# Block-sparse attention with a gated convolution feed-forward on one core: more buffers in eight pools, and another written-out order

## The chip, the cores and the metric

The kernel runs on one core of a Trainium2 chip. The metric is the device time of one execution in microseconds (us); lower is better. Three runs of the kernel before gave 210.2, 214.19 and 211.23 us, a median of 211.23 us.

## The reference

The input is q, k and v of shape (4, 8, 768, 64), a table of three random key blocks for each of the 24 query blocks, and the weights of a feed-forward layer. Cut to what matters:

```python
mask = (abs(blk_i - blk_j) <= 1) | first or last block | sampled blocks   # blocks of 32
scores = where(mask, q @ k.T / sqrt(64), -1e9)
attn = softmax(scores)                         # over the keys
x = (attn @ v) as (4, 768, 512)                # heads side by side
h = maximum(x @ w_in, 0)                       # 512 -> 1024
conv = sum over k of conv_w[k] * h shifted by k - 1 along the sequence
out = (h * sigmoid(conv)) @ w_out              # 1024 -> 512, float32
```

## The kernel before

The attention is computed densely: the mask comes in through 24 extra rows of the contraction (64 + 24 = 88 partitions), so that masked scores get a large negative term. Queries and keys are kept transposed in tiles `e` and `o` (the two heads of a pair, lines 326 and 328 for the copies into them). The scores of a unit, eight blocks of 128 by 128, are written by TensorE into one of two PSUM tiles `st` (L744). ScalarE takes their exponential into a tile `pt` (L755). TensorE multiplies `pt` with the values `vt`, which carry a column of ones, into one of two PSUM tiles `av` (L777). There are 144 such units. When a pair of heads has all its keys, VectorE takes the reciprocal of the row sums (L694) and normalizes into `xtok` (L696); a DMA transpose issued by SyncE (L705), or in a few places TensorE (L715), gives the transposed tokens `xT`.

The feed-forward runs on segments of 384 tokens (the last two of 256 and 128) between the units of later segments. TensorE multiplies `xT` with `winb` into a PSUM tile `mix` (L893). ScalarE (L913) or VectorE (L915) applies the relu into `hE`. VectorE does the convolution with per-partition weights `cw` (L947 and L957), ScalarE the tanh (L996), VectorE the gate `gT` (L999 and L1004). TensorE multiplies `gT` with `woutb` (L823; L808 for the last block), ScalarE (L326) or VectorE (L328) evicts into `o2s`, and a DMA writes the output (L831, L817). In the last segment the convolution is done on TensorE (L968) with diagonal matrices `diag` that VectorE writes (L388).

The loads of the first pair of heads come through SyncE and ScalarE in float32 and are cast (L238, then L326 or L328). All other loads of q, k, v and the large weights are issued by GpSimd, which converts while loading; a small copy named `pace` (L415 and L658) makes GpSimd wait for a unit's `pt` or for an earlier load. The pairs from number 5 on are transposed by DMA into `stg` (L583) and copied. The convolution weights are loaded as `cw0`, 24 rows of 128, by one small DMA (L238); TensorE transposes them (L378) and VectorE writes `cw` (L380).

The program is first built as a graph of operations, each with the engines that may do it and the pools from which it takes buffers. Then `put_down` reads the string `ORDER`. Each entry is two characters that number an operation, one for the engine where there is a choice, and one for each buffer that it takes:

```python
o = ops[64 * CODE.index(line[x]) + CODE.index(line[x + 1])]
...
for b in o.allocs:
    b.index = CODE.index(line[x])
```

So the string decides the order on every engine's queue, which engine does a copy, an eviction or a relu, and which buffer is used. Every engine runs its instructions in the order of its queue, and the waits between them follow from the data and the buffers.

Of the kernel before, what the change touches and what calls it, by code (L numbers as in the profile page):

```python
# [21 lines left out]
rmrnrorprqrrrsrtru0Y0rv1210ZA00XA0VA0+ArwrxryrzrArBrCrDrErFrGrH0/015110A16A0i0x13V14V0lV0jVrI4o017A0y0mV11V0B
0nA4prJrK4t14q04u1g11hV11j01lV1kV0q0p1dV01E21G31H1801m11S00O1U2461V0t0u0w0v4v11iV4y04z4D14E4A24I04J4F34K44r14s
4w4Q14R4S54x4B4C0s0r1rV14V04W4G1u01vV24+14/4X05011x11zV4H4L1yV4N0530544M05b15c4T0E15525d31wV0C0F1FV25g05h1I04U
5l14Y5i45m1JV34Z1L11KV5n51MV1NV4O5q05r19051525v15w565s05x1571TV30G5810J0N591bV1aV5e15D05E5f5j5k5o5I15J5F25p5t
1n15N05u5y5O5z05G0P470Q48241490R4a1A04b0S4c2604d274e0T4f2c24g1O14h2e14i2f4j2k04k2m34P05a4l2n4m5K35S15H5L5T5P4
5A25B5C1oV5U55/05M605Q6105R6415V5W656906a5X05Y25V41pV5Z05+V6616e16216fhr1ho06b26g36j0hp636khs0k0DhqV0htVhM06l4
6r1676s6t5hx0hyhzA6w06xhu1hv1B06y0hOhNhPhwVhQhU1hVhWhX6B16C686c6d6hhD16G0hE6H1CA1DA6D1hFAhA06i6m6n06O1hB1W16u
6P6v6z6I2hCAhRhY1XV46o1i021YV6pi16Q36T0hG06A6U6E6V4hH6F6Y16ZhJ16J6+56KhK710726R16S6WhZhLAhIA730i3hSi26L0i4hT0
i57611P1im06X6/1RV1QV777e01Z1707f747817j17k756M2806q1296Ni831+V1/Viah+2dV0h/i9ig17g27l37o07p797a07h7i7t17u7q4  # L30
i6ibi77b2ic7v5ih7B07C7D0id7m7n7r7s7G17w7x7Hin2lV12aV0io7L07M2g12h7I17N2ii7c7d7y12bV7z7E17Q17R7F7J7K7V07Wieifip
7O7S37A7X42s12u2v24n0IiqV0811827P7T7U860878358807Y7Z0ij8b18civ0iw8g08h7+02iV12jV2tV2ixV7/ikA1is1itiuViQ08d12o0
2p8i28o18p8q3iB08t0848uiC858v48y18z898a8e8f8D08E8j8kiy1iz8A58F12x2w2C2002F802iAAiRiSiTiDViU2qV2iV2rV8l2iY1iE0
8r18s8I18w8JiF8K0iGA8x8Q02118B8R8C8V18W8GiH0iI8H8S28X3iZi+22V8miW23Vi/8+08/904iXj0iJVj18LiK1iL931948M0iMVj42j5
8N1j7j28O8T9b08U8Y9ciN0iO8Z91iPVj39559g19h9d19i0jC19l09m9n3929697980jc3j6jdj8jfjejg999q19r9s59e19f9j9k9v09wjq0
9x19D19E9o9pjr9t9u9I0jD9y9J9z0j99F0jh9N19G9O9HjajbjijEjs9K59P02G02D22EV3jj2I2H2Q2N2R12O02y12z2J08n2K8P9a9S09T
jFjt9U2juA20L2LV39A2jGV32PV49B2MV2AV40K2BV9+19L9M9/a30a49QjI1jJa04jL0a819RjM9Va9a53jKA1jNA2/3032T2S2Yaa032ad0
aejU19Wa119X19YjX0k40jVai1a2jYaf1jWAk6jZVa6a7ajk11aq0abark2jO0acak2jPas5k5kk1k7kmjQAav1awaA0agahalaBjR0jSam0
ax4aC3k8k3Vklknan0j+1j/k0VkoaF1atjTAk9kc2aokdks3kfkakektkgkukb1aGaN0jk0auayaOaH0jlazaS1aTaP1kpaU5jw1jmaX0aYir
jHjv2U09C0il331aZ4khjxaDaEjnjoA0aIaJb01b1b23jyjzb50aQ1aRb6aVaWkA0jAA3b70kqaK22V2WV0kvkikwkjaLkxbd1a+bekG1a/b3  # L40
b4kBbi0bjkHb8b902Z131373820Map9Z34aMbf2bn1bo2XVkykrkCkzkD2+V0bk139V135V1bp536Vba0bb3a3b23f3c3d3ebs0kIbtkJkKV2
bA1kEA1kP0bBkQkM1kNkRVkOVl80l9lalblcbu4bC3bF0bGbgbhblbK1bLbmkS0bqbH0bM2bP0brbQkTbR1bU1kV1kWbVc00bvbwbD1bEc1ld
kUVkXVbx1lg2lhlelibyk/0bIbJbNbW5c23c51c6c70bOl0ca0cbbSbTbXbY0cf1cgkY1kZcc2ch5ljl1Vlklfk+VbZ2lllo13p3m3n03q03u
3r3g0bc1jp3hkFb+b/bzc3l20c4cn0cocp4l51l3l6cs1ctcx0l4Al7Acyc8c9lK0cdcecicjcu1cz3lplqlr3v1lw3lmlxlnlslylzcC1cD
cE0ltck0lAlucllvlE1cq1cH0lFcIcP1crcvcwcAcQcBcFlLcGcJ5cU0cKcL0cVlGlMlBcR4cW13s3E3t3B3F13J3G3H3C13I3Q3R2cmcScZ1
c+3iV2lClDlHlNd20d3cTc/2cXda1db3oV2lIV0cM2lOV1d43dc0m31cYd0m00d1m1m4cN3jVm2V0m5Adf0dgdk1dlm60m7dh5mo0mpm8Vdm4
mf1mgd5d6dp0dqdu1mc0mddr1meAmhAdd1jB3w3klP3K0cO23L3T3U33Y3V3W3Xdvdw2434403ldedC0dDml0mmm91mamnAdE3mr3xV4d71mq
3yVmsmE2dH1didImi0mjmFmGmbVmw1mxdJ0mkVmtd8djdM0dndodNlQ1dR1dSdslRdO5lSdtdxdZ0d+lTdT4mM3mHmz3DV3dz0mumydAmImv0
mAlUV3mNmOd/1e21e3dy0dFdGdKe70e42dLlW0lXdPdQe8ec1dUdVedmJmBe93lYlZe01m+1e1ee0mCdW2mDmPl+A1eh0eiej5e5e6m/eamU0
mVebep1eqeu0evmKmQdXmLmR3MV3mSmTn0mWn13Z1kL3+d93SV445V03/V0mXefegekdBlVdYl/3AlJer4ew1n2A2em13NVen40VmYA3ez1eA  # L50
eE0nd1eFeB2neeG3na0nbnfVncVnA0nBnCnDnE3PmZ3O3z41eo042eM1eNeO0el0n41eR0eSeT5n5n70n8eW1eseteXe/0exeyf0eCeDn6An9A
ns1eY4ng1nhf41eHeIf5nj0f11nFntnuniVeJ0nveKf62fc0nkfdfe3nwnlVnxnGnI2np1nqnJnrVnKnynLeP1fh1eQfinm0eUeVfm0eZfnnn
e+f2f3f7fj0fo5noAnznMnQ3nSnRnHf92nTfafr1f80fffsfgfkflfpfz0fAft4fB1nNnY1fE1fFo20fqfufvfJ0fKfG2fw1nUnOfL3nVfxnP
nZo3fR1fC1fDfHfSfIfMfW0fXfNn+o4fT0fY5eLfbfyf/1fU0g0nWg14nXo5o6V10Hg70g8n/fVfZgc1gdo0A0ok0olo7n3o1g91ge2fO0omV1
on1ooopVoI1oKgh0gioq0gp1gj3oJoLfPot1orosAgqouovAoQ0oRoToSgu0gvgr0oC0f+g2oF1oGoHAoDoEAgw5g3g42oUp42g5ga1gbgz1gA
oz1oAgfgggkglow0oxoBAgB4p5gm1oMgs0gnoyAoY3gtgxgyfQ1g6gogCgI0gJgDoNgN1gK1gOoe1ofogp6gE0gFoZo+gL1gG0gMgV0gP2gHV
o/oVp0oOoWohgQgWp7oP1gS2oiA3gR0po0ppgX3pqApA1gTp8h11h2pu1gYgZpvpx0pyh60h30pwApr1pspzAp1pBpCoXpQ0p2p3g+0pDg/ptA
p9papRpEpbpI3pJpLo80o9h7gU2h0hf1oaobhgh41h5h85ocA1pi1pjpkhh4plh9ha0hihjpc0pmA2pFhb1hchd1heAhk2pKhlpdpehm1pfpM
pNpgA0pGhnVqg1qhqiAqp0qqpHpY2pSpOpTqrAqj1qkqs1qtqm0qnqlAqu1qoAqx0qypPqz3pZp/pUpVp+qvq0phpnodojq1qa1qC1q40qDqH0
# [1001 lines left out]
```

## Time and profile before

| quantity | value |
|---|---|
| median of three runs | 211.23 us |
| span of the profiled execution, first to last instruction | 207.2 us |
| the profiled execution's own total time | not shown on the page; the median is 4.0 us above the span |
| TensorE busy | 196.7 us, 95% |
| ScalarE busy | 189.4 us, 91% |
| VectorE busy | 181.5 us, 88% |
| GpSimd busy | 60.7 us, 29% |
| granted TensorE clock | 1.000 |
| loads and stores | 26.26 MB, mean 127 GB/s |

Busy times are read with care. An instruction's time runs from its start to its end, and neighbours on one engine overlap by a little, so that the sum of busy times is more than the time that the engine needs. A matmul that is held up counts as busy too. In the rows of the profile, PE is TensorE's matmul, PEld its weight load, ACT is ScalarE, DVE VectorE, POOL GpSimd, SP SyncE; a q behind the name stands for the issue of a DMA. Rows of the timeline give the start, the duration, the engine, the line, the operation and the count of instructions that were merged; what stands in brackets is the idle time before and what ended it. The DMA share is the mean busy share of 16 DMA engines by the times of their packets, and it can exceed 1 where packets of several queues overlap on an engine.

### The profile page before, as it was taken

The numbers are of one execution on the slowest core, as the hardware profiler recorded it, in microseconds if no ns is written. First come the engines' busy times: TensorE is split into PE (matmuls) and PEld (weight loads), VectorE is DVE, ScalarE is ACT, GpSimd is POOL, SyncE is SP. The second block draws the span as 40 slices with busy tenths as digits, with TensorE's granted clock in tenths as the row PEclk, the third lists the DMA queues.
The fourth block names the chain that finished last, engine by engine and source line by source line (L and its number), as shares of the span: only waits on it lengthen the run. The fifth ranks groups of instructions, "written<-read, shape, count | busy, mean of one in ns | idle before, by whom it ended". The sixth has DMA issues, their size and how long they took to land.

```text
span 207.2 us, 6783 instructions
## 1 busy us (share of the span) xinstructions
PE 196.7 (95%) x2667; PEld 153.7 (74%) x2687; DVE 181.5 (88%) x571; ACT 189.4 (91%) x248; POOL 60.7 (29%) x113
## 2 busy tenths in 40 slices
PE   7799979989999999999999999999999999999993
PEld 7689858867878877777688767777688877795752
DVE  6877759999699998999999998999799959999950
ACT  6899969999999999999999998999899999998841
POOL 8844355446326124500605292700000000000000
...
GB/s 149 170 207 200 173 169 126 141 135 157 158 151 134 98 138 194 181 190 58 77 167 133 88 103 218 170 213 73 175 43 22 19 121 66 29 11 6 156 50 202
DMA packets 54903, 26.26 MB, mean 127 GB/s; under 512 B 40864, under 2 KB 51832, under 8 KB 54872
## 3 DMA queue, kind: packets, MB, share of 16 engines
...
## 4 chain that ended last, share of the span: by engine, by line
PE 56%; ACT 16%; DVE 16%; DMA 5%; issue 4%; SPq 0%; ACTq 0%
PE st L744 16%; PE mix L893 14%; PE mix L823 14%; ACT pt L755 12%; PE av L777 9%; DVE m L947 5%; DMA xT<-xtok 3%; DVE m L957 3%; DMA o2s<-in_q_dram 2%; DVE hE L915 2%; DVE xtok L696 2%; DVE gT L1004 1%; ACT hE L913 1%; DVE m L999 1%; DVE e L328 1%
## 5 line engine op out<-in xcount | busy, mean ns | idle before, releaser
L755 ACT ACTIVATE pt<-st 128x1024 bf16<-128x1024 f32 x144 | 140.2, 1036 | 5.4 <-PE st L744 5.0
L777 PEld LDWEIGHTS <-pt 128*128 128x128 bf16 x1152 | 53.1, 97 | 11.6 <-issue 0.2
L777 PE MATMUL av<-vt,pt 128*128 128x65 bf16 x1152 | 60.6, 193 | 0.3
L893 PE MATMUL mix<-xT,winb 128*128 128x384 bf16 (+2 forms) x288 | 53.8, 308 | 1.1 <-DMA xT<-xtok 0.9
L947 DVE TENSOR_SCALAR m<-hE,cw 128x382 bf16<-128x382 bf16 (+2 forms) x192 | 49.6, 317 | 0.2
L744 PE MATMUL st<-o 88*128 88x128 bf16 (+1 forms) x240 | 44.3, 229 | 1.1 <-ACT pt L755 0.8
L744 PE MATMUL st<-o,e 88*128 88x128 bf16 (+1 forms) x228 | 43.8, 233 | 0.5 <-ACT pt L755 0.4
L744 PE MATMUL st<-e,o 88*128 88x128 bf16 (+1 forms) x224 | 43.0, 234 | 1.2 <-ACT pt L755 1.2
L823 PE MATMUL mix<-woutb,gT 128*128 128x512 bf16 x156 | 43.1, 379 | 0.8
L744 PE MATMUL st<-e 88*128 88x128 bf16 (+1 forms) x208 | 41.5, 239 | 0.6 <-ACT pt L755 0.5
L744 PEld LDWEIGHTS <-o 88*128 88x128 bf16 x464 | 34.4, 97 | 9.4 <-issue 3.0
L744 PEld LDWEIGHTS <-e 88*128 88x128 bf16 x436 | 33.0, 97 | 7.5 <-issue 1.4
L957 DVE TENSOR_TENSOR m<-m 128x764 bf16<-128x764 bf16 (+2 forms) x64 | 33.8, 532 | 0.4
L893 PEld LDWEIGHTS <-winb 128*128 128x128 bf16 x288 | 23.9, 97 | 8.2 <-issue 1.6
L996 ACT ACTIVATE m<-m 128x764 bf16<-128x764 bf16 (+2 forms) x32 | 26.3, 826 | 0.5 <-DVE m L957 0.4
L415 POOL COPY pace<-pt 1x1 bf16<-1x1 bf16 x24 | 8.3, 347 | 47.3 <-ACT pt L755 47.0
L823 PEld LDWEIGHTS <-gT 128*128 128x128 bf16 x184 | 15.4, 97 | 9.0 <-DVE gT L1004 0.5
L915 DVE TENSOR_SCALAR hE<-mix 128x384 bf16<-128x384 f32 x29 | 15.9, 554 | 4.3 <-PE mix L893 4.1
L696 DVE TENSOR_TENSOR xtok<-av,rcp 128x384 bf16<-128x384 f32 (+2 forms) x36 | 18.2, 506 | 0.3
L1004 DVE TENSOR_TENSOR gT<-m,hE 128x764 bf16<-128x764 bf16 (+3 forms) x36 | 18.1, 508 | 0.3
L913 ACT ACTIVATE hE<-mix 128x384 bf16<-128x384 f32 (+2 forms) x35 | 16.9, 503 | 1.6 <-PE mix L893 1.2
L238 POOL DMA_DIRECT2D nat<-in_q_dram x23 | 16.9, 736 | 3.0 <-issue 2.8
...
## 6 DMA issues: line engine op xcount, KB each, us to landing
...
xT<-xtok SPq DMA_TRANSPOSE x32
```

Source lines behind the costliest of these rows:

```text
L696: nm = op("norm", {"DVE": t_dps(128 * C)}, lambda e: nc.vector.tensor_tensor(out=xtok_t[xk.index][:, 0:C].rearrange("p c h d -> p h c d"), ...
L744: nc.tensor.matmul(out=st[:, 128 * x:128 * (x + n_)], lhsT=QK[kc % 2][s][0:88, 1, hh, kc // 2, :], rhs=QK[par][s][0:88, 0, hh, idx:idx + n ...
L755: nc.scalar.activation(out=pt_t[ptb.index], in_=st_t[stb.index], func=AF.Exp, bias=0.0, scale=0.125)
L777: nc.tensor.matmul(out=o[:, off:off + 65], lhsT=pt_t[ptb.index][:, 128 * x:128 * x + 128], rhs=V_t[vslot_b[P].index][:, hh, kc, 0:65], sta ...
L823: nc.tensor.matmul(out=acc(), lhsT=gT_t[gb.index][:, ffc, 128 * t:128 * t + 128], rhs=woutb[:, ffc, :], start=(ffc == 0), stop=(ffc == NFF ...
L893: nc.tensor.matmul(out=mix_t[hb.index][:, w1 * y:w1 * y + w1], lhsT=winb[:, fc, 128 * ffc:128 * ffc + 128], rhs=xT_t[xt_buf[n].index][:, f ...
L913: i = nc.scalar.activation(out=dst, in_=src, func=AF.Relu, bias=0.0, scale=0.5)
L915: i = nc.vector.tensor_scalar(out=dst, in0=src, scalar1=0.5, scalar2=0.0, op0=ALU.mult, op1=ALU.max)
L947: i = nc.vector.tensor_scalar(out=m_t[cb.index][:, x, y, 0:w], in0=hE_t[heb.index][:, f0 + y, t0 + x:t0 + x + w], scalar1=cw[:, x, f0 + y: ...
L957: nc.vector.tensor_tensor(out=m[:, a_, :, 0:w], in0=m[:, a_, :, 0:w], in1=m[:, b_, :, 0:w], op=ALU.add)
L996: th = [op("tanh", {"ACT": t_act(2 * w) + 0.04}, lambda e, cb=cb, w=w: nc.scalar.activation(out=m_t[cb.index][:, 0, :, 0:w], in_=m_t[cb.in ...
L1004: i = nc.vector.tensor_tensor(out=gT_t[gtb.index][:, f0:f0 + 2, t0:t1], in0=m_t[cb.index][:, 0, :, 0:w], in1=hE_t[heb.index][:, f0:f0 + 2, ...
```

## The change

The numbers of buffers grow in eight pools: the staging tiles from 2 to 3, the load tiles `nat` from 4 to 6, `vn` from 3 to 4, `pt` from 6 to 8, `xtok` with its reciprocals from 3 to 4, `xT` from 3 to 4, and the output tiles `o2s` from 4 to 5. (The pool of `xtok` holds two tiles for each of its places, which makes eight kinds of tile.) The tiles of PSUM, the slots of `e`, `o` and `vt`, `hE`, `m` and `gT` keep their numbers. The string `ORDER` is another one; the operations that it names are the same ones. With it change the order on each queue and the engine of some operations: ScalarE has 9 evictions of 512 columns from `mix` and VectorE 13, where there were 15 and 7, and ScalarE has 24 relus of 384 columns where there were 27.

```diff
 ORDER = """
-040708090506000b1e00a0A0102030e0c0z0d0gV1f1c01q11s11t0WV20f0hA0oA0UAr21r3r4r5r6r7r8r9rarbrcrdrerfrgrhrirjrkrl
...
-qIqwpWpXqJ1qE0q2qAqBq3qM0qbqcq5qFq6q7qdqeA0q8A2qfq9qKqGqLqNqOqPqQA1qRAqS1qTqUqVqWV3qXSqY0qZq+q/r0Ar1A
+05040001020b0307r21r3180r40er508r6r7r8r9ra0a0zrb0hV1e00gArcrdrerfrgrh0Cri1f0oVrj06rkrl0A0crmrn0nA0drorp1c0rq
...
+qDq40pWq1pXqM0qE1q5q2qz0qKqLq6q3qcqAqFqBq7qGqdq8A0qNqeV2qOqS0qfqPodqTqUqQA1qVq9qY1qRAqWV3qZq+q/qXSr0Ar1A
 """
...
-    NSLOT, NSTG, NNAT, NVN, NPT, NXK, NXT, NHE, NCV, NGT, NOS = 5, 2, 4, 3, 6, 3, 3, 2, 4, 2, 4
+    NSLOT, NSTG, NNAT, NVN, NPT, NXK, NXT, NHE, NCV, NGT, NOS = 5, 3, 6, 4, 8, 4, 4, 2, 4, 2, 5
```

More of the change, by code (lines that the diff above doesn't have):

```diff
@@ L20 @@
 ORDER = """
-040708090506000b1e00a0A0102030e0c0z0d0gV1f1c01q11s11t0WV20f0hA0oA0UAr21r3r4r5r6r7r8r9rarbrcrdrerfrgrhrirjrkrl
[L22 to L59, printed above, removed]
-qIqwpWpXqJ1qE0q2qAqBq3qM0qbqcq5qFq6q7qdqeA0q8A2qfq9qKqGqLqNqOqPqQA1qRAqS1qTqUqVqWV3qXSqY0qZq+q/r0Ar1A
+05040001020b0307r21r3180r40er508r6r7r8r9ra0a0zrb0hV1e00gArcrdrerfrgrh0Cri1f0oVrj06rkrl0A0crmrn0nA0drorp1c0rq
@@ new lines @@
+0WA1rrrs0frtru0UArv1q1rwrx0i0XAry0Y0121rz1s2rA0ZA0rB0jVrC0/014A13VrD0lArE0+V1trF4o010A0VV4p0t0prG1E2rHrI4q0rJ
+rK1510B0y4t10mV1G34u0x16V0u1g117A0q4v14y01m14z0v11V1j01hV11H4A24D10w1kV4E1S31lV4F31dV04I01iV4J1U44r14s0r4w4K4
+4Q10O4R0s4x4B4C4S54G461rV14V01V4W1u04X60P4+11vV24/1x14H5074L1zV5301yV544M04T1wV4U5505b11FV25c474Y0k0Q4Z515d152
+5g04N05h4O1I15i2564P05l11JV35m1L01KV575n35e15q01NV5r5f1MV485j2405k5s45815v1595w5o0D5p5a1TV31915x55t5D01aV5E5u
+1bV1n05F65y5I15A25J5B5K71pV5N05C490R5O5z05G5H5P05S15T095L5M5U15Q0E15/00F600J5R6125V0G5W641655X35Y6636210N4a5Z1
@@ new lines @@
+1A0636901oV6a5+V6e16f6b44bho00Shphr16g5hqV0hs4c6j0265htV6khu0hM06l6hv6r1hO6s4d27hx1hNhwA67686t725V46w06xhPhyhQ
+6c6y01B04e6B1hzV0T6d6h6i1DV6mhR6C1CV6G04f2c1hD16o0hU16D1hE6p6HhA0hFV6I26q1hB6O1hV4g6n01O16PhX1W1hCA2806uhS6Q3
+6v6T01XV46UhJ0hW4h6V46z2e16A296Y11YV6Z6EhKhY6+54ihG12fhLV7106F6Ji02hZ721P04ji22k26K6R16S1RA7611QV736hHhT0771Z0
+hIV6W7877e0i832g17f4k2m06Xi16/707g0747j11/V7k1+V75792h6L17l14l6M2n7o07p7b37c7a07h7q27i4m7t1i36N2s37uig1i47v3
+7B0h+7Ci97d7m7n7r7D4ib7s7w7x7G1h/7H2o2i57y27L07z7Mim0ia7I5in2aV07Aihi67N6ic7E17F7J7Ki77Q12pid7R2bV7O7V0ii7S7ie
@@ new lines @@
+7W2dV0ioif7X07P8112lV1822iV1ij8312jV2u8602v287ikV07Tip8824n2008b1iqV18c7Uiv18d32x2tV28g02w8h2qV2iw8i47Yis07+0
+8o17/8pixAit2rV2C2D08t08q5iuV7Z02y08uiB1iQ0iy08v6iR8y18ziTiz8A7iCiS8D02z84iU858EiAA89iDV8I18F08a8JiY1iE0802i+
+iF8K12F8Q0iZ2G38RiH1i/8S2iIj08e8f8V1iGV8WiV8j2I8k2HiJV8+08r18/8X38l1j428s8w8x8B8m2108C904iK122V8n8G8H23V8L931
+iWj1948N38OiLiN0955iX8P9b09ciMV8M08T8U9d6j5iO8Yilj79g19hiPA2J1jC1j69i79l0j88Z9mj291922Kjc3969n0979q1j39e19f9r
+982jq0j9992Q2N9j2R49v0je9ajr9s1jd2O19w9kjf9o9p9x2jDjg9t9D1ja9ujh9Ejb9I09y9z09F39JjijEjjjs9A09K52AV3jF2U22EV3jt
@@ new lines @@
+jGV29G9H9N1juA39O2BV9S09T9P60IjI1jJjL09U4jKV19+19/9BjMa07jU1jNVa309L9Mk40a4jV2/0K305a50a81a9k5jX0jY0Maa1ad0jZV
+ae9Q9RjWA9Vk69W32a112Ta22Saf3k7ai1ajjO09X19Y2YjR12Z2ak6k8jSa631kk1aq0330arjTAjPkm37as4a7383j+1klj/jHjQVabk9ac
+agkc2av1awkeaA0k0Aahalkaax2aB2Vk10knam0k22LV4aC7ataF1kojvaGjw1kd9C3kpauaykfaN0jxk3AkgaOaH534kqjyan3kb1jk0aP0
+2PV4azjzkraDaEaoaIkhaS1aTks3apaX0jlaU1ktaYjAV4aJjmaZ39Z2MVjnb01aK2kib1joA0aQ1aLkG1b26kvaRaMb50b6kjaVkA0b74ku
+bd1kwkBkC35V0kx3a3b1be2+V0bi0aWbf2bjkya+kzkHkI0Lbk7bn12WV1boa/2XVkJbp53f3ckDkKV2bs03d39A1btkEV3bA1kP13g13ebu0
@@ new lines @@
+kQ36VbBkM0kRVbC1kN3mb3bF0kOVbGkV1l80bH3bK1b4l9bLb8kWlbbM6b90bglabP0bQlcbhkS0bR4ba0bU1kXVbVblkTbbbW2bm3pbq3n0
+kUVkY1bc0brc00lg1ld3q0c1kZlhc51c27ljl50c6libvbwk+Al6lkca0c75cblebD1bx3bEbyk/1cc0bIlfl0bzbJcf1l1VbNllbOcglo2bS
+bTirbXcn0l7Vch1bY0co3v2lml21lqc3cp3c4l3lnc8cs13hbZ1ctlpl4Ac9cx0cu6b+cdcycelw3cijpcjlE0cz4lrb/cC1ck2cDcllK1cE2
+ls3Ecq13ucH03F2cmlFlxltcIly3rlLlzcrcJ5cvcwcP1lAcAcBcQlulBcFlvcG3JcU03GcKcL0cR1cVlClG3HlDlMcM0cW73s3iV2lHcNlN3t
+cSlIV1cZ1lOA0c+d203jVd3c/3m90m01m1d46cTcXda1dbm2A0macYdc4df0mbV3wdgm31m4dh23Tdk13Bm5V3U3dld0d1mi0mo0dm53C1d53l
@@ new lines @@
+mjmpdp0mr3IdqmkAdu13K0mqd6dr1m613Q3Ymsdv3Vm73oV2dw0dd1ml0m8V3R2mmd73dC0d83WdDmnAmc13xV33zdE3dH13Xmdmw1dImM2de
+43di443djdJ6dn3L3DV3dodsmNdtdM0dNmxmeAmf03yVdxdO7lPmglQ1mz3Z1dR1mhAdSdZ0mtmE3dy0d+lJlW0mGdT4kFdFdz1lXmy3+lYd/2
+mAe21mue3dGmOdKmBdLkLdPdAlZcO1dQe45mv0dUdVe70mPe8lRmQe91d9ec1mClSmFedl+A0e01dW2lTdXdBee0eh0mHeie1e5lUV1m+0ej3
+dYep1mIe6eqeamDebmJeu0l/ef3MV4evegmRm/3OmKmLekmU1er63NVmVmSmWew7mTez1eA3/V1mXeB4em0enn0n1mYV3eE0eFn2V2na1eG2nb
+3SV4n3eM140VeN42nd0ncVeO5ne45V0eR0lVeSnfVn41eo2eT1nA0eW1eXnCn5el0eY0n70nB3ke/0nDf0n8n6AnEesjBf41f13n9Vf53Aetex
@@ new lines @@
+eyns1eCeDnFeHnteI3PeP1eQeUnveVeZf66fc041nGfdnj1nung0fe7eJ3nwnhnknHnxfh1finlVe+f2fm0fj4niVf3fnf7nI3np1fo2nqeK
+fr1nyfseLf80f91nrAfffanm0ft5fz0nKfAfgfbnzfkflfpfB1fqnJnnfunLfE1fFmZnoAnMfJ0fvfG0fC1o21fw2nQ2o3fxnNfKfR1nRfyfD
+fL3fHfSnSnY0nTfInZfT6nUfW0fMnOfNfXnVnPf/1g0fU0fY7n+nWnXfVo4g14o5g70o6V0g8n/fZf+o0V2gc1gdg2g3fO0ok1ge2fPolg43
+fQ30Hon0g95ooomV1gh1opVgiot1oI0gj1ouoq0oJorovAg5gp0oLgqosAg6gu1ga1oKgr0gvoC1oQ1gbgfggoRgw3gkoF0gloDgm1gz0gngs0
+oEAgtoSgogAoGoMgB6oz1oHVoAgxoTgyoNgI1ow0p43oxoBAp6gCgDgJoyAp5gN0gOgK7oY2oe1gE2ofgFgP4oZogohp7gG0p8gV1oiA1gL1gW
@@ L61 @@
+gHVh10p9o/ojh2pu1oUgX5pvpao+po0pwAp0ppgMoOoVgQh61oP1h7gR0pQ0pqAgYgZo81oWh32gS0o9oXpx0gTpA1p1gU0pypCh41hf0g+3
+pzAhgpBoag/h81p2obh0pDpr0pbocA4h5pspEo7p3pi1ptAo1pY3h9pjhh0hb1hcha0pkpRpThd0plpI2heAhihjpc0pmA3hk2hlpdpFpJhm1
+pepGhnApfpKpLqg1qhpgA1pMpZqiAphqp0p/pNqqpSpnqs1qtqrAqj1pHqkpUqH0qm0qlApOqnpPqu1qIqa1qvqJ2qwqbpVqoVqx1p+qyqC0q0
+qDq40pWq1pXqM0qE1q5q2qz0qKqLq6q3qcqAqFqBq7qGqdq8A0qNqeV2qOqS0qfqPodqTqUqQA1qVq9qY1qRAqWV3qZq+q/qXSr0Ar1A
 """
```

## The prediction

> **What bounds the kernel now.** I call the 144 exponentials of ScalarE (L755, one per group of eight score blocks) exp 0 to exp 143; they are the clock of the kernel. I first read the table of busy time by stretch, with the stretches cut where the waits changed.
>
> ```profile
> core 0: us, PE busy (x) PEld busy (x) DVE busy (x) ACT busy (x) POOL busy (x), PEclk, DMA share, GB/s
> 8.00:38.00 30.00, 26.54 (x430) 22.94 (x428) 23.52 (x72) 28.22 (x35) 14.33 (x29) 1.00 1.26 172
> 38.00:76.00 38.00, 36.68 (x554) 29.76 (x557) 35.40 (x104) 38.00 (x47) 16.18 (x28) 1.00 1.10 138
> 76.00:184.00 108.00, 107.25 (x1442) 81.73 (x1453) 101.08 (x303) 103.19 (x131) 23.09 (x42) 1.00 0.66 115
> 184.00:203.70 19.70, 19.36 (x184) 12.95 (x183) 15.51 (x63) 14.14 (x27) 0.00 (x0) 1.00 0.25 88
> 203.70:207.20 3.50, 0.01 (x1) 0.00 (x0) 0.00 (x0) 0.37 (x1) 0.00 (x0) 1.00 0.39 137
> ```
>
> ScalarE has no idle time at all from 38 to 76 us; from 76 us to 203.7 us TensorE has none worth the name (0.75 us in 108). So an early delay of ScalarE reaches the end in full, ScalarE work taken away before 76 us is gained in full, and what is taken from ScalarE later is worth little. The waits say where ScalarE lost time before 38 us, and that of the pools that grow only the value buffers held anyone up for long (Pool, 1.8 us).
>
> ```profile
> ACT pt L755 <- PE st L744: 5.0, 11, 1.6
> PE mix L893 <- DMA xT<-xtok: 0.9, 1, 0.9
> POOL vn L238 <- DVE vt L328: 1.8, 1, 1.8
> ```
>
> The longest, 1.6 us, stands at exp 22 in ScalarE's timeline: exps 0 to 21 run without a gap at 20.79/22 = 0.945 us each, then TensorE, in order, stands at the first feed-forward matmul (L893), whose transposed tokens xT are late.
>
> ```profile
> 8.57 20.79 ACT L755 ACTIVATE pt<-st 128x1024 bf16<-128x1024 f32 x22
> 25.38 3.97 ACT L755 ACTIVATE pt<-st 128x1024 bf16<-128x1024 f32 x4
> 30.91 1.02 ACT L755 ACTIVATE pt<-st 128x1024 bf16<-128x1024 f32 x1 [1.55 <-PE st L744]
> 33.10 1.05 ACT L755 ACTIVATE pt<-st 128x1024 bf16<-128x1024 f32 x1
> ```
>
> These give exp 0 at 8.57, exp 18 at 25.38, exp 22 at 30.91, exp 24 at 33.10.
>
> **The change, part by part.** No operation is added but two more clears of load buffers; TensorE issues as many instructions as before. I compared the listing of each engine's instructions in order, before and after. On TensorE the score groups, value matmuls, projections and output matmuls keep their mixture within about 1 us of work at every exp: nothing there moves the end. Four things differ.
>
> *1. The load of the second key half (k1).* Before, ScalarE issues it second of all. Now it stands behind the table load and two mask writes:
>
> ```text
> before ACT: DMACopy q0 | DMACopy k1 | LoadActFuncSet | 2 mask writes | ...
> after  ACT: DMACopy q0 | LoadActFuncSet | 2 mask writes (wait DVE) | DMACopy k1 | copy e | cast k0 | cast q0 | cast k1 | copy e<-mix | copy o<-mix | copy e<-e | copy e<-av | exp 0
> ```
>
> ```profile
> 0.74 0.42 ACTq L238 DMA_DIRECT2D o2s<-in_q_dram  x1
> 1.19 0.45 ACTq L238 DMA_DIRECT2D o2s<-in_k_dram  x1
> 1.67 1.28 ACT L296 ACT_TABLE_LOAD   x1 [1.67 <-PEq L1045]
> 2.97 0.61 ACT L296 ACTIVATE o<-nblk 24x128 bf16<-24x128 bf16 x2
> 5.11 0.51 ACT L326 CAST nat<-o2s 128x384 bf16<-128x384 f32 x1
> 6.50 0.47 ACT L326 COPY o<-mix 64x384 bf16<-64x384 bf16 x1
> 7.75 0.26 ACT L326 COPY o<-av 64x128 bf16<-64x128 bf16 x1
> 8.03 0.51 ACT L326 COPY e<-e 24x384 bf16<-24x384 bf16 x1
> 3.73 0.36 DVE L328 CAST nat<-o2s 128x384 bf16<-128x384 f32 x1 [0.62 <-DMA o2s<-in_k_dram]
> 1.67 4.43 DMA o2s<-in_q_dram
> 22.73 6.50 DMA xT<-xtok
> ```
>
> New issue: 1.19 + 1.28 + 0.61 = 3.1 us. How long it then takes is unknown. The first key half was issued at 0.74 (SyncE, below) and its cast began at 3.73 on the landing: 2.99 us, with the queues empty; the second query half took 4.43 us, when the Pool queue's loads had begun; a transposed token block at 22.7 took 6.50 us. k1 now starts with Pool's loads under way, as the 4.43 did: landing 7.5 us, bounds 6.1 and 9.6. Behind its cast stand the first copies of keys and masks: 0.51 + 0.47 + 0.26 + 0.51 brings the mask copy to 9.3. VectorE waits for that copy with a 24x1536 copy at the head of its queue; behind it stand another mask copy, a query copy, a second 24x1536 copy and, last, the key copy o<-av that exp 2 needs:
>
> ```profile
> 9.56 0.55 DVE L328 COPY o<-o 24x1536 bf16<-24x1536 bf16 x1
> 6.92 0.53 DVE L328 COPY o<-e 24x384 bf16<-24x384 bf16 x1
> 5.57 0.27 DVE L328 COPY e<-mix 64x256 bf16<-64x256 bf16 x1
> 7.50 0.36 DVE L328 COPY o<-av 64x384 bf16<-64x384 bf16 x1
> 16.05 0.60 PE st L744 x6
> ```
>
> 0.55 + 0.53 + 0.27 + 0.55 + 0.36 = 2.3, then the scores 0.60: exp 2 at 12.2, against 8.57 + 2 x 0.945 = 10.5. The start costs 1.8 us (0.4 to 3.9).
>
> *2. The load of the convolution weights (cw).* SyncE issued it at 2.07 us; now it stands behind the three first xT transposes, each of which waits for its normalized tokens. TensorE's cw transpose (L378) moves from before exp 10's scores to before those of exp 18, VectorE's L380 and six diagonal writes with it.
>
> ```profile
> 0.74 0.39 SPq L238 DMA_DIRECT2D o2s<-in_k_dram  x1
> 2.07 0.39 SPq L238 DMA_DIRECT2D cw<-in_moe_conv_w_dram  x1
> 20.46 4.97 SPq L705 DMA_TRANSPOSE xT<-xtok  x3
> 21.21 1.25 DVE L388 TENSOR_SCALAR diag<-ident,cw 128x128 bf16<-128x128 bf16 x6
> 16.71 0.24 PE L378 MATMUL mix<-ident,cw 24*128 24x24 f32 x1
> ```
>
> The three issues ended at 25.43. The third one's tokens need a value matmul that stands 1.5 exps earlier on TensorE (1.4 us) in a kernel that started 1.8 us later: issue ends at 25.8. A 12 KB load has no timed row at this place; by the 4.43 us it lands at 30.2, with bounds 2.99 and 6.50. I take the middle row since the DMA share of this stretch is 1.26, its queues loaded, while the 6.50 held a transposition of 96 KB. TensorE would reach L378 once exp 16 ends, at 8.57 + 17 x 0.945 + 1.8 = 26.4; it stands there, and behind it are the scores of exp 18 and the value matmuls. Exp 18 starts at 30.2 + 0.24 + 0.60 = 31.1.
>
> The Trainium skill says, in "DMA: Bandwidth & Descriptors", section "Queues, rings and completion order", that each DMA engine goes round-robin between queue rows a packet at a time, and takes one ring in order. By that rule cw would wait for the transposes ahead of it in SyncE's ring but hardly for Pool's loads, and the sum would be nearer its 2.99 us end; the 4.43 us of a 96 KB load beside Pool's first loads does not bear out so light a share.
>
> *3. What the cw wait absorbs.* By 31 us xT has landed, so the old stall at exp 22 goes. Six exps and one relu take 6 x 0.945 + 0.5 = 6.2 us: exp 24 at 37.3, if nothing follows. Something does: VectorE's diagonal writes (1.25 us for six) hold the normalization whose transpose stands before exp 20's scores, and twelve L893 matmuls crowd between those of exps 21 and 23; up to 1.1 us. I take 37.8, half of it: 4.7 us after the old 33.10 (4.2 to 5.3).
>
> *4. Work moved from ScalarE to VectorE.* Counting up to exp 60, ScalarE loses two relus of 384, one eviction and one 512-wide query copy; over the kernel six evictions and three such relus.
>
> ```profile
> L913 ACT ACTIVATE hE<-mix 128x384 bf16<-128x384 f32 x27 | 12.9, 505 | 0.8 <-PE mix L893 0.6
> L326 ACT COPY o2s<-mix 128x512 f32<-128x512 f32 x15 | 8.7, 592 | 3.3 <-PE mix L823 3.2
> L915 DVE TENSOR_SCALAR hE<-mix 128x384 bf16<-128x384 f32 x29 | 15.9, 554 | 4.3 <-PE mix L893 4.1
> L755 ACT ACTIVATE pt<-st 128x1024 bf16<-128x1024 f32 x144 | 140.2, 1036 | 5.4 <-PE st L744 5.0
> L328 DVE COPY o2s<-mix 128x512 f32<-128x512 f32 x7 | 4.8, 682 | 2.3 <-PE mix L823 1.6 <-PE st L744 0.7
> 60.00:80.00 20.00, 19.78 (x300) 15.93 (x301) 19.77 (x59) 19.95 (x25) 5.63 (x9) 1.00 0.90 134
> ```
>
> 2 x 0.505 + 0.592 + about 0.59 (as an eviction of that width) = 2.2 us, of which I take 2.0, since neighbours on ScalarE overlap (1.036 us for an exp that steps by 0.945). VectorE gets 6 x 0.682 + 3 x 0.554 = 5.8 us; between 76 and 184 us it has 7 us free. Cost nothing, covered by that slack; the cover is thin between 60 and 80 us.
>
> *The buffers themselves* (a third staging buffer, two more load buffers, two more for probabilities, one more for values, tokens, xT and outputs) remove waits off the path: Pool's 1.8 us passed with its loads not yet due. In TensorE's stage they can win at most the 0.75 us idle; I take 0.4.
>
> **Sum:** +4.7 - 2.0 - 0.4 = +2.3 on the span, 209.5 us. What lies around the span is the median less the span, 211.23 - 207.2 = 4.0; this execution's own total is not shown, so I add the 2.3 to the median: 213.5 us.
>
> **The rivals.**
>
> *A, slower: small loads of SyncE and ScalarE take as long as the transposes did.* At 6.50 us for both, k1 lands at 9.6, the start costs 3.9, the transposes end at 27.9 and cw lands at 34.4; exp 24 comes at about 35.3 + 6.2 = 41.5, +8.4, and the sum is +6.0: 217.2. For it: the DMA share above 1 up to 76 us. Against: cw is small. It decides (2%, 4.2 us) once the two latencies are 2 us longer together than I took.
>
> *B, faster: the loads are served between Pool's packets.* At 2.99 us the start costs 0.4; the transposes end at 25.43 + 0.4 - 1.4 = 24.4, cw lands at 27.4, exp 18 starts at 28.2, exp 24 at 34.4, +1.3; less 2.2 and 0.75, -1.7: 209.5. With cw ready at once, ScalarE has only +0.4, no stall at exp 22 (-1.6), -2.2 and -0.75: 207.1. For it: 2.99 us was measured; against: only with queues empty. The round-robin rule named above leads here.
>
> *C, VectorE becomes the bound from 57 to 80 us.* Busy 19.77 of 20 there, with an eviction and two relus more on it (1.8 us): late normalizations hold value buffers and TensorE. Added to my sum: 215.3. Against: instructions overlap on VectorE too, so its 19.77 us hold some free time.
>
> *D, the change doesn't do what it says:* both loads land in time, and ScalarE's 2 us turn into waits for TensorE, which was itself busy 36.68 of 38 us in that stage, with its mixture unchanged: 211.2. Against: ScalarE, busy 38.00 of 38, was the tighter of the two.
>
> **How the numbers follow.** Forecast 0.43, A 0.22, B 0.17, C 0.11, D 0.07. The range goes from 208.5, between B's two ends, to 218.0, a little beyond A; that leaves out B's far end and A with C on top. A measurement here can tell about 2% (4.2 us) from no change. Slower by over 2%: A, half of C and the forecast's tail, 0.30. Faster: the far end of B, 0.07. Within 2%: 0.63.
>
> **What would show it.** Right: exp 2 at about 12 us; TensorE waiting some 4 us at L378 for the load of cw, with ScalarE idle before exp 18; no wait for xT at exp 22; ScalarE without gaps to about 78 us; then TensorE full to the end. Wrong: no wait at L378 (B or D), VectorE the releaser of TensorE's scores between 57 and 80 us (C), or TensorE idle by microseconds after 80 us, which no term of mine has.

## The result: 4.5% slower

The changed kernel took 220.87 us (median, 220.48 to 221.36), the kernel before beside it 210.71 us; the ratio is 1.045, with a 95% interval of 1.037 to 1.053. The forecast was 213.5 us in a range to 218.0. The profiled execution has a span of 219.1 us and a total of 220.9 us, so that 1.8 us lie around the span.

The lag is the start of an exp less the start of the same exp in the profile before. In the changed kernel it is +0.4 at exp 0, +6.3 at exp 18, +6.3 at 24, +4.6 at 36, +6.2 at 48, +7.4 at 60, +8.6 at 72, +8.5 at 96, +9.7 at 120, +11.7 at 132 and +11.9 at the end. So there are two losses: one stall ahead of exp 18, and from exp 36 a slow leak of 7 us in all. The profile before is of a quick execution of its kernel (207.2 us of span against 209 that its median would have), so that lags to it stand 1 to 2 us above the differences of the medians; disturbed executions, some per cent longer, are left out of the times and ratios of the experiments.

**The stall.** The first view is ScalarE's timeline of the changed kernel; the columns are start, duration, engine, line, operation and count.

```profile
1.18 1.28 ACT L296 ACT_TABLE_LOAD   x1 [1.18 <-PEq L1045]
1.93 0.34 ACTq L238 DMA_DIRECT2D o2s<-in_k_dram  x1
6.36 0.51 ACT L326 CAST nat<-o2s 128x384 bf16<-128x384 f32 x1 [1.95 <-DMA o2s<-in_k_dram]
...
10.55 15.99 ACT L755 ACTIVATE pt<-st 128x1024 bf16<-128x1024 f32 x17
31.72 1.02 ACT L755 ACTIVATE pt<-st 128x1024 bf16<-128x1024 f32 x1 [5.19 <-PE st L744]
33.24 1.02 ACT L755 ACTIVATE pt<-st 128x1024 bf16<-128x1024 f32 x1 [0.49 <-PE st L744]
```

k1 landed 4.43 us after its issue, and exps 1 to 17 ran without a gap; then ScalarE stood for 5.19 us. The reason stands on SyncE's queue and on TensorE's timeline:

```profile
19.28 5.89 SPq L705 DMA_TRANSPOSE xT<-xtok  x3
25.22 0.55 SPq L238 DMA_DIRECT2D cw<-in_moe_conv_w_dram  x1
...
30.39 0.27 PE L378 MATMUL mix<-ident,cw 24*128 24x24 f32 x1 [4.43 <-DMA cw<-in_moe_conv_w_dram]
30.78 0.31 PE L744 MATMUL st<-e 88*128 88x128 bf16 x1
```

The 12 KB of cw were issued behind the three transposes, from 25.22 to 25.77, and landed at 30.39: 5.17 us after the start of their issue, 4.6 us after its end. TensorE stood for 4.43 us at one transpose of 24 rows, and all scores stood behind it.

**The leak.** The table by stage, cut where the three stages of the profile before were, each moved by its lag (to exp 27, to exp 60, and on to some exps before the last):

```profile
8.40:42.90 34.50, 29.30 (x427) 25.64 (x426) 23.51 (x75) 26.95 (x31) 17.28 (x36) 0.86 1.21 164
42.90:83.30 40.40, 38.63 (x577) 30.28 (x573) 39.17 (x109) 38.36 (x47) 9.92 (x21) 1.00 1.14 132
83.30:195.50 112.20, 110.00 (x1455) 82.04 (x1454) 104.25 (x305) 102.54 (x127) 22.23 (x42) 1.00 0.60 103
```

The second stage took 38.0 us before and 40.4 now; ScalarE, which had no idle time in it, has 2.0 us. The third took 108 us and takes 112.2; TensorE, which had 0.75 us idle in it, has 2.2. VectorE is the engine whose busy time rose most in the second stage, from 35.4 to 39.2 us (TensorE's rose from 36.7 to 38.6). The granted clock was 1.00 in both stages, so the leak is not one of clock. For whom they wait stands in the table of waits (engine, line, what it waited for: us in total, times, longest), where VectorE's gate gT and its convolution sums m have taken places that hardly showed before (0.5 us for gT):

```profile
ACT pt L755 <- PE st L744: 11.8, 15, 5.2
DVE cw L380 <- PE mix L378: 6.4, 1, 6.4
PEld L823 <- DVE gT L1004: 6.4, 15, 1.0
DVE hE L915 <- PE mix L893: 5.7, 4, 2.8
ACT m L996 <- DVE m L957: 5.5, 10, 0.9
```

The chain that ended last is made of VectorE as much as of TensorE: in the profile before VectorE had 16% of it.

```profile
PE 42%; DVE 40%; DMA 9%; issue 4%; ACT 2%; POOL 0%; SPq 0%; ACTq 0%; DVEq 0%; POOLq 0%
```

### The profile page after: what moved, and what is told of

Read it like the earlier page. It is cut to its first block, busy times and chain, and to the rows that moved or that the text cites. A ratio compares the mean times of both kernels' runs of the same rounds, so it can differ in the third digit from the quotient of the medians.

```text
span 219.1 us, 6795 instructions
## 1 busy us (share of the span) xinstructions
PE 202.9 (93%) x2687; PEld 155.2 (71%) x2687; DVE 189.7 (87%) x583; ACT 186.6 (85%) x238; POOL 56.9 (26%) x113
## 4 chain that ended last, share of the span: by engine, by line
PE 42%; DVE 40%; DMA 9%; issue 4%; ACT 2%; POOL 0%; SPq 0%; ACTq 0%; DVEq 0%; POOLq 0%
PE st L744 13%; DVE m L947 11%; PE mix L823 10%; PE mix L893 9%; DVE m L957 8%; PE av L777 6%; DVE hE L915 4%; DVE xtok L696 4%; DVE gT L1004 3%; DMA vn<-in_v_dram 3%; DMA xT<-xtok 2%; DMA cw<-in_moe_conv_w_dram 2%; DVE m L999 2%; DVE o L328 2%; DMA o2s<-in_k_dram 2%
## 5 line engine op out<-in xcount | busy, mean ns | idle before, releaser
L777 PEld LDWEIGHTS <-pt 128*128 128x128 bf16 x1152 | 53.2, 98 | 11.7 <-issue 1.5
L893 PE MATMUL mix<-xT,winb 128*128 128x384 bf16 (+2 forms) x288 | 54.8, 308 | 1.2 <-DMA xT<-xtok 0.7
L823 PE MATMUL mix<-woutb,gT 128*128 128x512 bf16 x176 | 47.6, 380 | 2.2 <-DVE gT L1004 1.8
L744 PE MATMUL st<-o 88*128 88x128 bf16 (+1 forms) x240 | 45.1, 233 | 0.5 <-ACT pt L755 0.4
L744 PE MATMUL st<-o,e 88*128 88x128 bf16 (+1 forms) x228 | 44.6, 238 | 0.3 <-ACT pt L755 0.3
L744 PE MATMUL st<-e 88*128 88x128 bf16 (+1 forms) x208 | 42.7, 244 | 0.8 <-DVE e L328 0.5
L744 PEld LDWEIGHTS <-e 88*128 88x128 bf16 x436 | 34.3, 99 | 10.1 <-issue 2.5
L957 DVE TENSOR_TENSOR m<-m 128x764 bf16<-128x764 bf16 (+2 forms) x64 | 34.4, 538 | 1.2
L823 PEld LDWEIGHTS <-gT 128*128 128x128 bf16 x184 | 14.6, 97 | 13.8 <-DVE gT L1004 6.4
L415 POOL COPY pace<-pt 1x1 bf16<-1x1 bf16 x24 | 6.6, 274 | 63.8 <-ACT pt L755 63.5
L915 DVE TENSOR_SCALAR hE<-mix 128x384 bf16<-128x384 f32 (+1 forms) x33 | 17.9, 548 | 6.1 <-PE mix L893 5.7
L913 ACT ACTIVATE hE<-mix 128x384 bf16<-128x384 f32 (+2 forms) x31 | 15.2, 498 | 1.2 <-PE mix L893 1.2
```

The lines of the kernel that those rows point to most:

```text
L744: nc.tensor.matmul(out=st[:, 128 * x:128 * (x + n_)], lhsT=QK[kc % 2][s][0:88, 1, hh, kc // 2, :], rhs=QK[par][s][0:88, 0, hh, idx:idx + n ...
L777: nc.tensor.matmul(out=o[:, off:off + 65], lhsT=pt_t[ptb.index][:, 128 * x:128 * x + 128], rhs=V_t[vslot_b[P].index][:, hh, kc, 0:65], sta ...
L823: nc.tensor.matmul(out=acc(), lhsT=gT_t[gb.index][:, ffc, 128 * t:128 * t + 128], rhs=woutb[:, ffc, :], start=(ffc == 0), stop=(ffc == NFF ...
L893: nc.tensor.matmul(out=mix_t[hb.index][:, w1 * y:w1 * y + w1], lhsT=winb[:, fc, 128 * ffc:128 * ffc + 128], rhs=xT_t[xt_buf[n].index][:, f ...
L915: i = nc.vector.tensor_scalar(out=dst, in0=src, scalar1=0.5, scalar2=0.0, op0=ALU.mult, op1=ALU.max)
L957: nc.vector.tensor_tensor(out=m[:, a_, :, 0:w], in0=m[:, a_, :, 0:w], in1=m[:, b_, :, 0:w], op=ALU.add)
```

## The experiments

The edits are entries of `ORDER` that are moved, or engines of entries; the diffs name the operations. Profiles of e1 to e4 count lines one higher from `ORDER` on. "V", "S", "B", "P" are the names that the expectations give to the theories. The differences below are medians against the kernel before on the same chip; the lags are each read from one profile.

**Early load of cw, in the changed kernel (e1).**

```diff
 ld_q0     (SyncE, second query half)
+ld_cw     (SyncE, convolution weights)
 ...
 xb        (SyncE, third xT transpose)
-ld_cw
```

> The changed order, with one entry moved: the load of the convolution weights cw is issued by SyncE at the start, after the second query half, as it was before. Theory W (three separate losses that add up: about 1.3 us at the start, about 5 us at TensorE's wait for cw, about 5 us later on VectorE): the wait at L378 and ScalarE's 5.2 us gap before exp 18 go, a short wait for xT at exp 22 may come back; 215 to 217 us. Rival G (the cw wait is refilled, because something else, xT or the normalization, would have held TensorE there anyway): less than 2 us gained, 219 to 221 us. Rival L (later stages only look late because the early stall displaced loads and transposes): more than 8 us gained, below 213 us.

It took 215.7 us, +6.1, ratio 1.028 (1.021 to 1.036). The lag is +1.1 at exp 24 and -0.4 at exp 36: the stall is gone. Then it is +3.5 at exp 60, +4.6 at 96, +6.8 at 132, +7.1 at the end. The late load costs 4 to 5 us (10.2 - 6.1 by the medians, 11.9 - 7.1 by the lags); the leak is a matter of its own. Its waits:

```profile
PEld L824 <- DVE gT L1005: 6.4, 15, 1.0
ACT m L997 <- DVE m L958: 5.3, 10, 0.9
PE mix L824 <- DVE gT L1005: 2.9, 8, 0.8
```

**k1 early too (e2).**

```diff
 ld_q0     (ScalarE, first query half)
+ld_k0     (ScalarE, k1)
 table load, mask writes
-ld_k0
```

> As the kernel with cw early, and the second key half is loaded by ScalarE before its table load, as before. Theory W: exp 2 comes near 10.4 us again and the time is 1 to 1.5 us below that of the kernel with cw early, 214 to 216 us. Rival: the start is covered, since VectorE's backlog of copies behind the mask copy sets exp 2 anyway: the same time as with cw early within 0.5 us.

216.75 us, ratio 1.035 (1.028 to 1.042), no better than e1. Exp 2 came 0.4 us earlier than in the profile before, where e1 had it 0.6 later and the changed kernel 1.3, but at exp 24 e1 and e2 both stood at +1.1. The late start is absorbed.

**One order to exp 60, the other after it (e3: the change first; e4: the kernel before first), both in the larger pools.**

```diff
 entries of ORDER up to exp 60: those of one kernel
-the rest in its own order
+the rest in the order of the other kernel
```

> The changed order up to exp 60, then all remaining operations in the order of before, with the engines of before, in the larger pools. Theory W: it keeps the 7.4 us that the changed kernel has lost by exp 60 and loses nothing more: 217 to 218.5 us. Rival L (the later loss is a consequence of the early one): about 220.5 us. Rival P (TensorE catches up once it is no longer held): below 215 us.

> The order of before up to exp 60, then all remaining operations in the changed order, with its engines, in the larger pools. Theory W: no loss by exp 60, and then the 4.5 us that the changed kernel loses after it: 214 to 216 us. Rival L: about 211 us, since nothing early is displaced.

e3 took 217.84 us, ratio 1.041 (1.034 to 1.048): lag +6.5 at exp 60 and +7.4 from exp 96 to 143. e4 took 213.97 us, +4.4, ratio 1.025 (1.015 to 1.034): -0.1 at exp 60, +2.5 at 96, +4.7 at 132. So the changed order loses 4.7 us after exp 60 even behind an undisturbed start, and the order of before, behind the changed start, loses only 0.9. The waits of e4 have the same sign as the leak:

```profile
PEld L824 <- DVE gT L1005: 4.5, 12, 0.5
ACT m L997 <- DVE m L958: 3.9, 9, 0.8
```

**The engines put back, and the engines alone (e5: e1 with every relu and eviction on its engine of before; e6: the order of before with the engines of the change, 22 relus and 8 evictions).**

```diff
 relu (64), ev (25): the engine letter of the entry
-that of the kernel's own ORDER
+that of the other kernel's ORDER
```

> The changed order with cw loaded early, and every relu and every output eviction done by the engine that did it before (15 evictions and 27 relus of 384 on ScalarE again), at its place in the changed order. Theory V (the loss from exp 36 on comes from the work moved to VectorE): 210 to 212.5 us, against 215.7 us with cw early alone; VectorE's busy time between exp 36 and exp 60 falls. Theory O (it comes from the order in which VectorE, TensorE and ScalarE take the same work, so that one engine stands at the head of its queue while its other work is ready): 214.5 to 218 us. In part each: 212.5 to 214.5 us.

> The order and pools of before, with every relu and every output eviction on the engine that the changed order gives it (nine evictions and 24 relus of 384 on ScalarE). Theory V: 213 to 216 us, most of the 5 us that are lost with cw early. Theory O: 208.5 to 211.5 us, no change from before beyond an eviction that comes a little earlier or later.

e5: 218.84 us, ratio 1.040 (1.031 to 1.048), no faster than e1 (1.028, 1.021 to 1.036). e6: 226.45 us, ratio 1.072 (1.060 to 1.084), the lag growing from 0.6 at exp 30 to 10.7 at exp 96 and 12.8 at the end. Both are slower than either theory had it. The engines of the change in the order of before cost much; the engines of before in the changed order win nothing. That an order and its engines belong together is a reading of this.

**The larger pools alone (e7).**

```diff
-    NSLOT, NSTG, NNAT, NVN, NPT, NXK, NXT, NHE, NCV, NGT, NOS = 5, 2, 4, 3, 6, 3, 3, 2, 4, 2, 4
+    NSLOT, NSTG, NNAT, NVN, NPT, NXK, NXT, NHE, NCV, NGT, NOS = 5, 3, 6, 4, 8, 4, 4, 2, 4, 2, 5
```

> The larger pools with the order of before, which names only the buffers that there were: the tiles lie at other places in SBUF and the extra ones are not used, but for the clears of two more load buffers. Both theories: no change, 209 to 211.5 us. A rival that blames the place of the tiles in memory: 213 us or more.

211.22 us, ratio 1.004 (0.993 to 1.014): no difference that shows. The order of before names only the buffers that there were, so this run tests where the tiles lie, and not the use of the added buffers.

**The late load alone, in the kernel before (e8).**

```diff
-ld_cw     (SyncE, fourth load); cw_t, cw, diag ahead of exp 10
 xb        (SyncE, third xT transpose)
+ld_cw     and cw_t, cw, the first three diag groups ahead of the scores of exp 18
```

> The kernel before with one thing of the change: the cw load is issued behind the first three xT transposes, and TensorE's L378, VectorE's L380 and the first nine diagonal writes stand directly ahead of exp 18's scores, as in the changed order. Theory W (the wait for cw costs what it delays ScalarE): a gap of 3.5 to 5.5 us before exp 18, of which the old wait for xT at exp 22 gives back about 1.2 us; 212.5 to 214.5 us. Rival: the early loss is caught up by exp 60: below 211.5 us.

215.21 us, ratio 1.021 (1.014 to 1.028). The lag is +5.6 at exp 18 and +5.3 at each exp looked at from 24 to the end: what is lost before exp 24 reaches the end in full, and without the new order nothing leaks.

```profile
ACT pt L755 <- PE st L744: 10.4, 13, 6.0
DVE cw L380 <- PE mix L378: 5.9, 1, 5.9
PE mix L378 <- DMA cw<-in_moe_conv_w_dram: 5.6, 1, 5.6
```

**Less and more work on VectorE in the order of before.** e9 moves 15 diagonal writes (2.4 us) from exps 41 to 132 into VectorE's gaps at 24 and 28 us. e10 adds 36 diagonal writes into a tile that nobody reads, 12 (2.0 us) in each of three stretches, at exps 38 to 44, 84 to 90 and 110 to 116:

```diff
+    spare = sb.tile([128, 128], BF16, tag="spare", name="spare")
+    for _ in range(12):
+        def more(e):
+            for x in range(3):
+                nc.vector.tensor_scalar(out=spare, in0=ident, scalar1=cw[:, x, 0:1], scalar2=None, op0=ALU.mult)
+        op("extra", {"DVE": 3 * t_d4(128)}, more, 0, [o_cw, o_ident])
```

> The kernel before with five of its eight groups of diagonal writes (15 writes at 0.163 us a step, 2.4 us, that stand after exps 41, 63, 77 and 132) moved on VectorE to its two gaps before the first relus, about 24 and 28 us. Theory V (VectorE has no slack to speak of from exp 36 on, so its work there is paid in full): exp 96 comes about 1.9 us earlier, 208 to 210 us where before gives about 211. Theory S (the slack that the prediction counted exists): no change within 0.7 us.

> The kernel before with 36 more diagonal writes into a spare tile, twelve each (2.0 us) spread over exps 38 to 44, 84 to 90 and 110 to 116. Their result is used by nothing. Theory V: the lag behind the kernel before rises by about 2 us at each of the three places and stays; 215 to 217 us. Theory S: they are covered by 7 us of VectorE's idle time between 76 and 184 us; the lag rises by less than 0.7 us at each place, 211 to 213 us.

e9: 210.41 us, ratio 1.002 (0.997 to 1.006), as S has it. e10: 216.3 us, +6.6 for 6.0 us of work, ratio 1.029 (1.020 to 1.038), as V has it; its lag grows from 2.6 at exp 38 to 3.9 at 62, from 3.9 at 88 to 6.1 at 98 and from 6.1 at 108 to 8.6 at 120, and nowhere else after exp 36. Of the 2.0 us added at the first place VectorE's slack took 0.7, at the other two nothing; and work taken from it won nothing. That the other engines stand at their limits too would explain the second; no run shows it.

**One order to exp 36, the other after it (e11: e1 first; e12: the kernel before first).**

```diff
 entries of ORDER up to exp 36: those of one kernel
-the rest in its own order
+the rest in the order of the other kernel
```

> The changed order with cw early up to exp 36, then all that is left in the order of before, in the larger pools. Up to exp 36 it should run as the changed kernel with cw early did, 0.4 us ahead of before, with two gates of the first segment less done. Theory B (the loss between exps 36 and 60 is that backlog on VectorE): 3 to 4 us are lost by exp 60 all the same, 213 to 216 us. Theory O (it is the changed order after exp 36): little is lost, 209.5 to 212 us.

> The order of before up to exp 36, then all that is left in the changed order, in the larger pools. Theory B: no loss by exp 60, then the 4.7 us that the changed order lost when it took over at exp 60: 214 to 216 us. Theory O: another 3 to 4 us between exps 36 and 60, 217 to 220 us.

e11: 213.85 us, ratio 1.018 (1.013 to 1.023); lag +0.2 at exp 36, +3.2 at 60, +4.0 from 96 on. e12: ratio 1.030 (1.016 to 1.044); only the ratio is read. Up to exp 36 the changed order has done one of the three first gates that the kernel before has done by then; behind that start even the order of before loses 3 us by exp 60, which fits a backlog of gates. e12 has no such backlog and its ratio is near that of e1 (1.028); but e4, whose changed order begins at exp 60 only, has 1.025, and the intervals are too wide to tell whether e12 loses anything between exps 36 and 60.

**The evictions alone.** e14 is e1 with only the evictions on their engines of before; e15 is the kernel before with only the seven evictions moved to VectorE.

```diff
 e14, e1:          ev (25): -engine of the change   +engine of before
 e15, kernel before:  ev (7):  -ScalarE                +VectorE
```

> The changed kernel with the load of the convolution weights early, and with every eviction of 512 columns on the engine of the kernel before (ScalarE 15, VectorE 7, instead of 9 and 13); the relus and the order stay those of the change. The kernel with the early load alone took 215.7 us, +7.1 us at the end against the profile before. Theory V (the amount of VectorE's work costs): six evictions of 0.68 us leave VectorE, 4.1 us, so about 212 us (211 to 213), and TensorE's wait for the gate goes down from 6.4 us. Theory S (the order costs, the engine hardly matters): 215 to 217 us, the same wait, ScalarE busier by 3.6 us.

> The kernel before, with its order and buffers, and only the seven evictions that the change gives to VectorE moved there from ScalarE: 7 x 0.68 = 4.8 us more on VectorE, 7 x 0.59 = 4.1 us less on ScalarE. Theory V (extra work on VectorE is paid in full): +4 to +5 us, 215 to 216 us, the lag growing at each moved eviction. Theory S (the order costs, the amount alone little): 211 to 212 us. My forecast of the record (the slack of VectorE after 76 us covers it): 210.5 to 211.5 us.

e15: 215.71 us, +5.3, ratio 1.028 (1.018 to 1.039). Seven evictions of 0.683 us are 4.8 us, and the 4.1 us that ScalarE is rid of bring nothing. The groups of e15 show the move:

```profile
L328 DVE COPY o2s<-mix 128x512 f32<-128x512 f32 x14 | 9.5, 683 | 4.8 <-PE mix L823 4.8
L326 ACT COPY o2s<-mix 128x512 f32<-128x512 f32 x8 | 4.7, 589 | 2.6 <-PE mix L823 2.5
```

e14: 216.78 us, ratio 1.032 (1.022 to 1.043), where e1 had 1.028. Taken from VectorE in the changed order, the same work wins nothing. So the amount is paid in full in the order of before, and it is not what bounds the changed order; there the wait for the gate stayed (6.0 us for the weight loads, 6.4 in e1).

**Where the consumers of VectorE's convolution stand.** The chain of a segment is convolution (VectorE), tanh (ScalarE), gate (VectorE), output matmul (TensorE), eviction. e16 moves the entries of 21 tanhs of e1 later, of which 16 come behind one or two more exps on ScalarE's queue; e17 moves the output matmuls, evictions and stores later as well; e18 moves the output matmuls, evictions and stores of the kernel before earlier; e19 moves the entries of 15 tanhs of the kernel before earlier, of which 12 pass an exp.

```diff
 e16, e1:          tanh                 +up to two exps later
 e17, e1:          tanh, f2, ev, out    +up to two exps later
 e18, kernel before:  f2, ev, out          +up to two exps earlier
 e19, kernel before:  tanh                 +up to two exps earlier
```

> The changed kernel with the load of the convolution weights early, and with 21 tanhs moved later on ScalarE's queue alone, each by up to two exps, so that they stand as far behind VectorE's convolution as they do in the kernel before (mean distance in the order 2.1 score groups in the change, 3.4 before, 4.0 here). The kernel with the early load alone: 215.7 us, ScalarE waiting 5.3 us for VectorE's convolution. Theory P (consumers stand too close behind VectorE, in order, and hold up what is behind them): the wait goes to about 1 us and the time to 212 to 214 us. Theory B (VectorE itself is late, whatever stands where): 215 to 217 us, the wait turns up at TensorE's output matmuls.

> The same with the output matmuls, their evictions and stores moved later too, each by up to two exps (60 of 88 matmuls). Theory P: TensorE's wait for the gate goes from 6.4 us to under 2, and the time to 209 to 212 us, equal to the kernel before or better. Theory B: 215 to 217 us, with the wait somewhere else.

> The kernel before with its output matmuls, evictions and stores moved earlier by up to two exps (74 of 89), VectorE's amount of work unchanged. Theory P: TensorE waits for the gate 4 us or more (0.5 before) and the time is 213 to 216 us. Theory B: 211 us, within 1.

> The kernel before with 15 tanhs moved earlier on ScalarE's queue alone, by up to two exps (mean distance behind VectorE's convolution 1.8 score groups, 3.4 before, 2.1 in the change). Theory P: ScalarE waits 3 us or more for the convolution (0.4 before) and the time is 212.5 to 215 us. Theory B: 211 us, within 1.

The consumers closer, in the order of before: e18 took 229.0 us, ratio 1.081 (1.074 to 1.089), and e19 222.61 us, ratio 1.048 (1.040 to 1.056). P has the sign and not the size (213 to 216 and 212.5 to 215 us). In e18 TensorE waits for the gate 10.7 us at its weight loads (0.5 before) and 7.8 us at its matmuls, partly the same time, and VectorE for the tanh:

```profile
PEld L823 <- DVE gT L1004: 10.7, 10, 2.4
DVE m L999 <- ACT m L996: 8.1, 10, 1.1
PE mix L823 <- DVE gT L1004: 7.8, 9, 2.5
```

The consumers further, in the changed order: e16 took 220.39 us, ratio 1.041 (1.035 to 1.047), and e17 229.99 us, ratio 1.086 (1.080 to 1.093), both slower than e1 and than either theory had it. Here P fails. In e16 the wait that was aimed at went from 5.3 to 1.7 us, as P has it; it came back one and two stations on:

```profile
PEld L823 <- DVE gT L1004: 8.6, 14, 1.1
DVE m L999 <- ACT m L996: 4.7, 7, 1.4
PE mix L823 <- DVE gT L1004: 4.6, 7, 0.8
ACT m L996 <- DVE m L957: 1.7, 3, 0.8
```

VectorE now stands 4.7 us in order for the late tanhs (not at all in e1), so the gates are late, and TensorE's waits for them went from 6.4 to 8.6 us and from 2.9 to 4.6. In e17 the wait of the weight loads for the gate is down to 1.1 us, and VectorE waits instead for the output matmuls that it evicts, and TensorE's feed-forward matmuls for those evictions, since both take the two `mix` tiles:

```profile
DVE o2s L328 <- PE mix L823: 11.1, 10, 2.6
PE mix L893 <- DVE o2s L328: 4.8, 8, 0.8
```

## Why the prediction was wrong

*1, the start: right in its row, and it doesn't reach the end.* k1 was 4.43 us on the way, the duration taken. Its issue came at 1.93 and not at 3.1, beside the table load. Exp 2 started at 11.68 (12.2 forecast). e2 shows that this delay doesn't reach the end.

*2, the load of cw: right in its mechanism, and to 0.2 us by luck.* It landed at 30.39 (30.2 forecast), and TensorE stood at L378 as forecast; its wait there, 4.43 us, answers to the 4 us named as the sign. But two errors cancel: the issue began at 25.22 and not at 25.8, and from there the load took 5.17 us and not 4.43 (e8: 4.64, from 24.82 to 29.46). Exp 18 came at 31.72 in the place of 31.1. e1 and e8 give this step 4 to 5 us from both sides. The Trainium skill's round robin between queue rows ("DMA: Bandwidth & Descriptors", "Queues, rings and completion order"), by which cw would have been nearer to 2.99 us, isn't borne out as a light share by the 5.17 and 4.64 us. No run here shows whether the transposes ahead or the other queues took that time.

*3, what it absorbs: right in kind, 1.6 us short at exp 24.* +6.3 was measured there, +4.7 forecast with +5.3 as the upper bound; ScalarE waited for TensorE three more times up to exp 22, by 0.49, 0.59 and 0.45 us, of which the last section speaks. 1.4 us were given back by exp 27 (+4.9), where the old order had gaps; that +4.9 is close to +4.7 is luck. In e8 the lag goes from +6.3 at exp 20 to +5.3 at exp 22, so a part of the old stall is swallowed, and the rest is never made up.

*4, the moved work and the order behind it: here the forecast failed, with its sign.* The prediction took 2.0 us off for ScalarE up to exp 60, let VectorE's 5.8 us "cost nothing, covered by that slack", and put no cost on the new order after exp 24, since on TensorE the mixture is the same to about 1 us: "nothing there moves the end". From exp 27 to 60 the lag rose by 2.5 us, from +4.9 to +7.4, where a fall of 2.0 was forecast; after exp 60 it rose by 4.5 where a fall of 0.4 was forecast. These two make 9.4 of the 9.6 us by which +11.9 missed +2.3.

The slack wasn't there, and the 2.0 us weren't won: in the order of before, 2 us of extra work in each of two stretches within 76 to 184 us cost 2.2 and 2.4 us (e10), and seven evictions moved cost 5.3 us for 4.8 us of work, with nothing back for ScalarE (e15). But this isn't what the changed kernel loses by: with the evictions, or all the work, back on their engines of before it is no faster (e14, e5). The larger fault is the other premise. "Nothing there moves the end" compared how much work each engine has by each exp, and not where each consumer stands behind its producer on another engine; e18 and e19 show what such places are worth at the same amounts, 17 and 11 us for up to two exps, and e4 has the new order lose 4.7 us of lag behind an undisturbed start.

*The buffers:* forecast at -0.4, too little for these runs to tell. e7 has no difference within its interval, and it doesn't use the added buffers.

*The rivals.* C (VectorE the bound between 57 and 80 us, +1.8) named the engine that the waits point at, but it is too local, since the leak runs from exp 36 to 132, and its cause, the amount of work on VectorE, is not borne out by e14 and e5. A and B were decided by the landing of cw and k1, which fell between them. D's first half, that both loads land in time, is refuted by the stall; its second, that ScalarE's 2 us turn into waits for TensorE, fits the 2.0 us that ScalarE is idle in the second stage. The last sign of being wrong, TensorE idle by microseconds after 80 us, came: 2.2 us in the third stage.

*What stays open.* Of the 10 us between the medians about 4 to 5 are the late load (e1 and e8), shown by putting it in and taking it out. About 6 are the new order (e1), in two places, exps 36 to 60 and after 60 (e1, e3, e4 and e11). The backlog at exp 36 would explain the first (e11), and e12 doesn't decide it. They are not the amount of work on VectorE (e14, e5), though the amount alone would cost as much in the order of before (e15, e10). That they are the places of the operations relative to each other follows from what is left. Which operations, no run tells: moving tanhs or outputs as a whole made it worse both ways. The choice of buffers, which `ORDER` also writes down, was not varied on its own. No version here beats the kernel before; e7 and e9 equal it.
